# Attention feeding a mixture of experts: key splits, routing groups, softmax sums and filler matmuls rearranged

## The chip, the cores and the metric

The kernel runs on one core of one Trainium2 chip. The metric is device time in microseconds (us), the median of the timed runs; lower is better. The engines are PE (TensorE: matmuls; their weight loads are listed as PEld), DVE (VectorE), ACT (ScalarE), POOL (GpSimd) and SP (SyncE, which here only issues DMAs).

## The reference, cut to what matters

Random-feature attention (batch 4, 8 heads, sequence 576, head width 64, 128 features), whose output goes, as 2304 rows of 512, to a mixture of experts with one expert for each token (8 experts, hidden width 1024, at most 576 tokens for each expert).

```python
def phi(x):
    proj = einsum('bhsd,df->bhsf', x, w_phi)
    proj = proj - max(abs(proj), axis=-1, keepdims=True)
    return concatenate([exp(proj), exp(-proj)], axis=-1)
q_p, k_p = phi(q), phi(k)
kv = einsum('bhsf,bhsd->bhfd', k_p, v);  z = sum(k_p, axis=2)
num = einsum('bhsf,bhfd->bhsd', q_p, kv)
den = einsum('bhsf,bhf->bhs', q_p, z)[..., None] + 1e-06
x = (num / den).transpose(0, 2, 1, 3).reshape(2304, 512)

logits = x @ w_gate
expert_idx = argmax(logits, axis=1)
probs = exp(logits - max);  probs /= sum(probs) + 1e-09
gate_w = probs[arange(N), expert_idx]
# tokens of an expert in order of their number, at most `capacity` of them
h = maximum(einsum('ecd,edf->ecf', disp, w1), 0.0)
y = einsum('ecf,efd->ecd', h, w2)
out[i] = gate_w[i] * y[expert_idx[i], pos[i]]       # zero for tokens beyond capacity
```

## The kernel before, in words

**Attention.** The tokens are done in two halves (p = 0, 1) of nine blocks of 128 tokens. For each half there are 18 key items (head group g = 0, 1 of four heads, times nine blocks r), then 18 query items (block times head group). `attention` runs them as a software pipeline written out by hand: at step t, stage i of item t - i, in the order of stages 0, 2, 3, 1, then waiting folds, then 4 to 7. A key item: projection on PE (`project`), subtraction of the largest magnitude on DVE (`center`: a reduce at L198 and a subtraction at L202), two exponentials on ACT (`k_exp`, L239 and L240), sums over tokens on PE (`kv_sum`, L292), and after the last block of a sequence a fold of the sums. A query item: projection, `center`, transpose and two exponentials, the numerator and denominator on PE (`q_num`, L339), and for every second item `rows_out`, which divides by the denominator on DVE and writes the block's 128 rows of 512 into a tile xr, and the logits into a tile lg.

**Inputs of the projections.** Keys and queries come in chunks of 640 or 512 columns for a pair of heads (hp = 0 to 3). `x_load` issues a chunk's DMA on SP; `x_split` turns it into two f16 parts: ACT makes the high part (L167), POOL the rest by a subtraction (L168) one step later. The first four key chunks of head pairs 0 and 1 are used unsplit. `plan(chunks, marks)` gives each chunk a step, its mark: in that step its split is put into ACT's line, and one further chunk is loaded, in the order of a list whose first two loads are issued ahead of the loop, one at a time. SP issues DMAs in order; they take turns on eight semaphores, so that each waits for the one eight before it. In steps 3 to 26 SP also issues two DMAs a step that fill the expert buffer xs with a constant tile (`fill_xs`, L134 and L137), and from step 30 those that fill the output.

**Routing.** Blocks are routed in groups: when the last block of a group has its logits, `route` appends a list of 20 small steps to `pending`: sum of the logits over heads (L436), largest logit, one-hot choice of the expert, exponential (ACT), running counts (rb), positions within the expert by matmuls (PE, L417), the softmax sum (L448, L449: smx), the gate as its reciprocal, the slot number si, and the scatters. `tick`, which `center` and `rows_out` call between their operations, does one of these steps each time (more when many wait). Scatters of finished rows to xs in HBM are indirect DMAs on POOL (L421), one a step. Scratch for routing lies partly in SBUF tiles, partly in one PSUM bank, sm_t (`quick`), that also holds positions and folds. The last block's multiplication (block 17) is put into its group's list as an eleventh step.

**Seam and experts.** When nothing is pending any more, PE sums the counts, DVE writes cnt, and `warm(48)` (L214) issues 48 filler matmuls whose result is not used; the profile shows each as two passes. Then, in program order: load of expert 0's rows from xs (`load_x`, L623, five DMAs that wait for all scatters), `prep` of its first two tiles of 128 rows (PE transposes at L639, high part on ACT at L640, low part on DVE at L641), the splits of its first weights (`w_split`, eight parts, L111 on ACT and L112 on DVE; the weights were loaded during attention), and the eight experts. `ffn1` does for each of eight 128-column pieces f of the hidden layer twelve matmuls on 256 rows: four high by high (L650) and four low by high (L651) in turns, then four high by low (L653). `relu`, `ffn2` and a scaled scatter of the result into the output (`put`, L695 on POOL) follow; later experts' rows and splits are prepared during the one before.

Of the kernel before, what the change touches and what calls it, by code (L numbers as in the profile page):

```python
# [8 lines left out]
F32 = mybir.dt.float32  # L9
# [6 lines left out]
ALU = mybir.AluOpType  # L16
# [21 lines left out]
def tile_kernel(ctx: ExitStack, tc: tile.TileContext, qT, kT, vv, w_phi, w_g, w1, w2, out, cap):  # L38
# [84 lines left out]

    POS, SCR = 4 * GC, 4 * GC + 24
    sm_t = ps_1.tile([P, 512], F32, tag="sm", name="sm")
# [219 lines left out]
    grp = [None]  # L345

    def rows_out(p, r):
        blk = p * NBLK + r
        i, n = next((blk - g0, n) for g0, n in groups if g0 <= blk < g0 + n)
        if i == 0:  # L350
            grp[0] = (r_p.tile([P, n, XW], F32, tag=f"xr{n}", name="xr", bufs=(1, 1, 3)[n - 1]),
                      r_p.tile([P, n, H, NE], F32, tag="lg", name="lg", bufs=2))
        xr, lg = grp[0]
        num = num_t.pop((p, r))[:, :, 0:4 * GC].rearrange("p g (h c) -> p g h c", c=GC)
        rd = r_p.tile([P, 2, 4, 1], F32, tag="rd", name="rd")
        nc.vector.tensor_scalar(rd, num[:, :, :, D:VC], 1e-6, None, ALU.add)
        tick()
        nc.vector.reciprocal(rd, rd)
        tick()
        nc.vector.tensor_tensor(lg[:, i].rearrange("p (g h) e -> p g h e", g=2), num[:, :, :, VC:GC],  # L360
                                rd.to_broadcast([P, 2, 4, NE]), ALU.mult)
        if i == n - 1:
            route(blk - i, n, xr, lg)
        if blk == NT // P - 1:
            warm(8)
        else:
            tick()
        rows = xr[:, i, 0:DM].rearrange("p (g h d) -> p g h d", g=2, h=4)
        if blk == NT // P - 1:
            pending[-1].insert(10, lambda: nc.vector.tensor_tensor(  # L370
                rows, num[:, :, :, 0:D], rd.to_broadcast([P, 2, 4, D]), ALU.mult))
        elif p == 0 or r >= 7:
            nc.vector.tensor_tensor(rows, num[:, :, :, 0:D], rd.to_broadcast([P, 2, 4, D]), ALU.mult)
        else:
            nb = r_p.tile([P, 2, 4, D], F32, tag="nb", name="nb", bufs=2)
            nc.scalar.activation(nb, num[:, :, :, 0:D], AF.Copy)
            nc.gpsimd.tensor_tensor(rows, nb, rd.to_broadcast([P, 2, 4, D]), ALU.mult)
        tick()

    def route(blk, n, xr, lg):  # L380
        def small(name, shape, dt=F32):
            return r_p.tile([P, n, *shape], dt, tag=name, name=name)

        k = next(k for k, (g0, _) in enumerate(groups) if g0 == blk)
        room = [SCR + 96 * (k % 2)]

        def quick(w, each=n):
            a = room[0]
            room[0] += each * w
            assert room[0] <= SCR + 96 * (k % 2 + 1)  # L390
            return sm_t[:, a:room[0]].rearrange("p (n a) -> p n a", a=w)

        lt, sh, ix, sl, rn = quick(NE), quick(NE), quick(1), quick(1), quick(NE, 1)
        mx, ef = small("mx", [1]), small("ef", [NE])
        oh = small("oh", [NE], BF16)
        rb = r_p.tile([P, NE], BF16, tag="rb", name="rb")
        es, sel = small("es", [NE]), small("sel", [NE])
        sm, pr, ov = (small(x, [1]) for x in ("smx", "pr", "ov"))
        si = r_p.tile([P, n], I32, tag="si", name="si")
# [28 lines left out]
        def run_total():  # L428
            if old is None:
                v.tensor_copy(rb, rn[:, 0])  # L430
            else:
# [5 lines left out]
            lambda: v.tensor_reduce(flat(mx), lt, AX.X, ALU.max),  # L437
            lambda: v.tensor_tensor(sh, lt, mx.to_broadcast([P, n, NE]), ALU.subtract),
            lambda: v.scalar_tensor_tensor(ef, sh, 0.0, io, ALU.is_ge, ALU.mult),
            lambda: v.tensor_reduce(flat(ix), ef, AX.X, ALU.min),  # L440
            lambda: v.tensor_tensor(oh, ix.to_broadcast([P, n, NE]), io, ALU.is_equal),
            lambda: (v if late else nc.gpsimd).tensor_copy(xr[:, :, XW - 1:XW].bitcast(I32),
                                                           tokid[:, blk:blk + n].unsqueeze(2)),
            lambda: nc.scalar.activation(es, sh, AF.Exp),
            lambda: v.tensor_reduce(rn[:, 0], oh.rearrange("p n e -> p e n"), AX.X, ALU.add),
            run_total,
            positions,
            lambda: v.tensor_reduce(flat(sm), es, AX.X, ALU.add),  # L448
            lambda: v.tensor_scalar(sm, sm, 1e-9, None, ALU.add),  # L449
            lambda: v.tensor_tensor(sel, pos[0], oh, ALU.mult),  # L450
            lambda: v.reciprocal(xr[:, :, DM:DM + 1], sm),
            lambda: v.tensor_reduce(flat(pr), sel, AX.X, ALU.add),
# [6 lines left out]

    groups = [(0, 3), (3, 3), (6, 3), (9, 3), (12, 3), (15, 2), (17, 1)]  # L460

# [50 lines left out]
    def attention():  # L512
# [9 lines left out]
        order += [(K, 0, hp, 1) for hp in (0, 1)]  # L522
        plan([(K, 0, hp, c) for c in range(2) for hp in (2, 3)], [3, 5, 7, 9])
        plan([(Q, 0, hp, 0) for hp in range(4)], [10, 12, 13, 15])
        plan([(Q, 0, hp, 1) for hp in range(4)], [17, 19, 21, 23])
# [61 lines left out]
        nc.vector.tensor_scalar(cnt, tot, float(cap), None, ALU.min)  # L587
        warm(48)
        return cnt
# [176 lines left out]
    load_x(0)  # L766
    for t in ahead:
        prep(0, *t)
    for c in range(2):
        for part in range(4):  # L770
            w_split(0, c, part)
    prep_gi(0)
    for e in range(NE):
# [44 lines left out]
```

## Time and profile before

| | |
|---|---|
| timed runs | 477.46, 475.06, 474.16 us, median 475.06 us |
| profiled execution | 478.01 us, of which the span of instructions is 476.3 us |
| mean granted TensorE clock | 0.982 |
| busy share of the span: PE, DVE, ACT, POOL | 93%, 59%, 51%, 32% |
| bytes moved | 81.88 MB, mean 172 GB/s |
| chain that ended last, by engine | PE 53%, DVE 2%, DMA 2%, others 1% or less |

The page of the profile gives one execution. Attention lies from 0 to about 193 us, the experts from about 205 us to the end. A timeline row gives the start, the duration, the engine, the line, the operation with its output and inputs, how many instructions of it follow each other without a gap (x), and in brackets the engine's idle time before it and what ended that. PEclk is the granted TensorE clock as a share of full speed.

### The profile page before, as it was taken

What the parts mean: (1) busy time and instruction counts of PE and PEld (TensorE: products, weight loads), DVE (VectorE), ACT (ScalarE), POOL (GpSimd) and SP (SyncE); (2) the same over time, 40 slices, a digit from 0 to 9 for tenths busy, and PEclk for the clock granted to TensorE, in tenths of its full rate; (3) what the DMA queues carried; (4) which work ended last, traced back from release to release, by engine and by line L of the source; (5) the groups of instructions that cost most, each with busy time, mean ns of one, the idle gap of its engine ahead of it and who ended that gap; (6) DMA issues with size and microseconds to landing.
All of it is one profiled execution on the core that took longest, in us unless ns stands there. A gap on an engine that the chain in (4) does not pass through costs nothing.

```text
span 476.3 us, 11047 instructions
## 1 busy us (share of the span) xinstructions
PE 444.6 (93%) x4297; PEld 370.4 (78%) x4297; DVE 279.0 (59%) x621; ACT 244.6 (51%) x456; POOL 154.2 (32%) x181
## 2 busy tenths in 40 slices
PE   6599999988999999889899999999999999999993
PEld 4356688864557887879888979898989897989891
DVE  6256668998766888157742536666757570466121
ACT  3548766677775554057632425565656551454211
POOL 3449734679881426230211012121212120010101
PEclk9899999999999999889999999999999999999998
DMA  7986898842956002558762038495958570000000
GB/s 214 263 249 193 243 301 260 267 135 77 341 189 233 1 26 95 180 174 331 232 253 80 4 135 309 141 354 159 343 170 316 190 265 25 24 24 7 23 23 27
DMA packets 41993, 81.88 MB, mean 172 GB/s; under 512 B 3775, under 2 KB 6463, under 8 KB 41920
## 3 DMA queue, kind: packets, MB, share of 16 engines
q1 hardware_dynamic: 38816, 71.47, 46.2%
q0 software_dynamic: 3104, 9.46, 5.2%
q8 instruction: 43, 0.70, 0.6%
q14 instruction: 30, 0.25, 0.2%
HBM read 57.27 MB, written 24.30 MB: 171 GB/s over the span
## 4 chain that ended last, share of the span: by engine, by line
PE 53%; DVE 2%; DMA 2%; issue 1%; SPq 1%; ACT 1%; POOL 1%; another core or an unknown queue 0%; POOLq 0%; ACTq 0%
PE ph L650 9%; PE ph L651 9%; PE ph L653 9%; PE py L681 7%; PE py L682 7%; PE py L683 7%; PE pt L639 2%; PE py L679 1%; PE py L677 1%; DMA xi<-xs 1%; SPq L623 1%; DMA xs<-xr,si 1%; POOL xs L421 0%; DVE xl L641 0%; DVE l L112 0%
## 5 line engine op out<-in xcount | busy, mean ns | idle before, releaser
L650 PE MATMUL ph<-xh,h 128*128 128x256 f32 (+2 forms) x352 | 90.2, 287 | 5.0 <-ACT xh L640 1.6
L112 DVE TENSOR_TENSOR l<-raw,h 128x512 fp32r<-128x512 f32 x128 | 84.1, 690 | 13.1 <-ACT h L111 7.4
L651 PE MATMUL ph<-xh,l 128*128 128x256 f32 (+2 forms) x352 | 90.2, 287 | 0.7 <-DVE l L112 0.5
L695 POOL DMA_INDIRECT out<-y,it x22 | 23.6, 1073 | 195.6 <-ACT h L111 99.8
L168 POOL TENSOR_TENSOR stk<-px,stk 64x1280 f16<-64x1280 f32 (+1 forms) x28 | 66.5, 2377 | 43.2 <-ACT stk L167 33.2
L111 ACT ACTIVATE h<-raw 128x512 fp32r<-128x512 f32 x128 | 74.3, 626 | 0.0
L650 PEld LDWEIGHTS ph<-xh,h 128*128 128x128 f32 x352 | 68.0, 193 | 6.6 <-ACT xh L640 3.5
L667 DVE SCALAR_TENSOR_TENSOR h<-ph,h 128x256 fp32r<-128x256 f32 (+1 forms) x112 | 38.4, 360 | 53.8 <-ACT h L664 53.7
L651 PEld LDWEIGHTS ph<-xh,l 128*128 128x128 f32 x352 | 68.0, 193 | 1.7 <-DVE l L112 1.5
L664 ACT ACTIVATE h<-ph 128x256 fp32r<-128x256 f32 (+2 forms) x88 | 33.3, 379 | 60.7 <-PE ph L653 49.9
L198 DVE TENSOR_REDUCE m<-pr 128x4 f32<-128x512 f32 x72 | 49.5, 687 | 20.5 <-PE pr L188 11.4
L681 PE MATMUL py<-h,h 128*128 128x512 f32 x152 | 60.1, 395 | 0.0
L682 PE MATMUL py<-l,h 128*128 128x512 f32 x152 | 59.3, 390 | 0.0
L683 PE MATMUL py<-h,h 128*128 128x512 f32 x152 | 59.3, 390 | 0.0
L653 PE MATMUL ph<-xl,h 128*128 128x256 f32 (+2 forms) x352 | 57.3, 285 | 0.0
L202 DVE TENSOR_TENSOR d<-pr,m 128x512 f32<-128x512 f32 x72 | 49.8, 692 | 7.8 <-ACT kp L240 4.1
L653 PEld LDWEIGHTS ph<-xl,h 128*128 128x128 f32 x352 | 49.3, 193 | 0.0
L641 DVE TENSOR_TENSOR xl<-pt,xh 128x512 fp32r<-128x512 f32 (+1 forms) x23 | 14.3, 653 | 55.7 <-ACT xh L640 42.0
L292 PE MATMUL acc<-kp,v 128*64 128x256 f32 (+1 forms) x320 | 40.5, 401 | 5.2 <-ACT kp L240 4.9
L339 PE MATMUL acc<-kv,qp 128*64 128x73 f32 x1152 | 44.4, 229 | 0.0
L339 PEld LDWEIGHTS acc<-kv,qp 128*64 128x64 f32 x1152 | 39.1, 136 | 5.9 <-issue 5.4
L640 ACT ACTIVATE xh<-pt 128x512 fp32r<-128x512 f32 (+1 forms) x23 | 12.1, 568 | 59.0 <-PE pt L639 28.5
(103 smaller groups left out, 691.3 us busy)
## 6 DMA issues: line engine op xcount, KB each, us to landing
raw<-in_w SPq DMA_DIRECT2D x32, 1024.0 KB, 7.5
xi<-xs SPq DMA_DIRECT2D x32, 257.0 KB, 5.1
xs<-fill SPq DMA_DIRECT2D x24, 257.0 KB, 5.8
out<-fill SPq DMA_DIRECT2D x18, 256.0 KB, 6.5
xs<-fill SPq DMA_DIRECT2D x24, 128.5 KB, 5.3
px<-in_kT SPq DMA_DIRECT2D x10, 256.0 KB, 6.7
px<-in_qT SPq DMA_DIRECT2D x8, 320.0 KB, 5.0
v<-in_vv SPq DMA_DIRECT2D x1, 2304.0 KB, 13.4
```

The costliest lines, as they stand in the source:

```text
L111: nc.scalar.activation(hi[:, part], t[:, part], AF.Copy)
L112: nc.vector.tensor_tensor(lo[:, part], t[:, part], hi[:, part].bitcast(F32), ALU.subtract)
L168: return lambda: nc.gpsimd.tensor_tensor(t[D:P], x, t[0:D], ALU.subtract)
L198: nc.vector.tensor_reduce(m.rearrange("p a b -> p (a b)"), pr, AX.X, ALU.max, apply_absolute_value=True)
L202: nc.vector.tensor_tensor(d, pr, m.to_broadcast([P, 4, NF]), ALU.subtract)
L339: nc.tensor.matmul(num[lo:hi, g, j * GC:(j + 1) * GC], qp[:, a, j, lo:hi], kv_t[b][:, a, 4 * g + j], start=(a == 0), stop=(a == 1))
L650: nc.tensor.matmul(acc, hi[:, k, fs], xh[:, k, o:o2], start=(k == 0), stop=False)
L651: nc.tensor.matmul(acc, lo[:, k, fs], xh[:, k, o:o2], start=False, stop=False)
L653: nc.tensor.matmul(acc, hi[:, k, fs], xl[:, k, o:o2], start=False, stop=(k == 3))
L681: nc.tensor.matmul(py[0:m], h_t[f][:, s0:s0 + m], hi, start=(f == 0), stop=False)
L682: nc.tensor.matmul(py[0:m], h_t[f][:, s0:s0 + m], lo, start=False, stop=False)
L683: nc.tensor.matmul(py[0:m], h_t[f][:, at:at + m], hi, start=False, stop=(f == 7))
```

## The change

Six edits, all in the kernel's body:

1. The marks of the first half's split chunks move: keys from steps 3, 5, 7, 9 to 5, 6, 8, 10, the first four query chunks from 10, 12, 13, 15 to 11, 12, 14, 15. The loads that hang on them move too.
2. Routing groups of the first half (blocks 0 to 8) are 4 and 5 blocks instead of 3, 3 and 3. All blocks of a half write their rows into one tile; the logits' tiles are named by group size.
3. In `route`, the softmax sum goes from an SBUF tile (smx) to the PSUM scratch (sm); the shifted logits overwrite the logits (sh is gone); the reciprocal stands ahead of the product with the one-hot.
4. Block 17's rows are multiplied by ACT, one operation for each head, instead of one DVE operation.
5. The eight splits of expert 0's first weights stand ahead of its rows' `prep`.
6. 28 filler matmuls instead of 48.

```diff
-    POS, SCR = 4 * GC, 4 * GC + 24
+    POS, SCR, SW = 4 * GC, 4 * GC + 40, 80
...
+    xr_t = r_p.tile([P, NBLK, XW], F32, tag="xr", name="xr", bufs=1)
...
-            grp[0] = (r_p.tile([P, n, XW], F32, tag=f"xr{n}", name="xr", bufs=(1, 1, 3)[n - 1]),
-                      r_p.tile([P, n, H, NE], F32, tag="lg", name="lg", bufs=2))
+            grp[0] = (xr_t[:, blk % NBLK:blk % NBLK + n],
+                      r_p.tile([P, n, H, NE], F32, tag=f"lg{n}", name="lg", bufs=2 if n == 3 else 1))
...
         if blk == NT // P - 1:
-            pending[-1].insert(10, lambda: nc.vector.tensor_tensor(
-                rows, num[:, :, :, 0:D], rd.to_broadcast([P, 2, 4, D]), ALU.mult))
+            for h in range(H):
+                nc.scalar.activation(rows[:, h // 4, h % 4], num[:, h // 4, h % 4, 0:D], AF.Copy,
+                                     scale=rd[:, h // 4, h % 4])
...
-        lt, sh, ix, sl, rn = quick(NE), quick(NE), quick(1), quick(1), quick(NE, 1)
+        lt, ix, sl, rn, sm = quick(NE), quick(1), quick(1), quick(NE, 1), quick(1)
...
-        sm, pr, ov = (small(x, [1]) for x in ("smx", "pr", "ov"))
+        pr, ov = small("pr", [1]), small("ov", [1])
...
-            lambda: v.tensor_tensor(sh, lt, mx.to_broadcast([P, n, NE]), ALU.subtract),
+            lambda: v.tensor_tensor(lt, lt, mx.to_broadcast([P, n, NE]), ALU.subtract),
...
             lambda: v.tensor_reduce(flat(sm), es, AX.X, ALU.add),
             lambda: v.tensor_scalar(sm, sm, 1e-9, None, ALU.add),
+            lambda: v.reciprocal(xr[:, :, DM:DM + 1], sm),
             lambda: v.tensor_tensor(sel, pos[0], oh, ALU.mult),
-            lambda: v.reciprocal(xr[:, :, DM:DM + 1], sm),
...
-    groups = [(0, 3), (3, 3), (6, 3), (9, 3), (12, 3), (15, 2), (17, 1)]
+    groups = [(0, 4), (4, 5), (9, 3), (12, 3), (15, 2), (17, 1)]
...
-        plan([(K, 0, hp, c) for c in range(2) for hp in (2, 3)], [3, 5, 7, 9])
-        plan([(Q, 0, hp, 0) for hp in range(4)], [10, 12, 13, 15])
+        plan([(K, 0, hp, c) for c in range(2) for hp in (2, 3)], [5, 6, 8, 10])
+        plan([(Q, 0, hp, 0) for hp in range(4)], [11, 12, 14, 15])
...
-        warm(48)
+        warm(28)
...
     load_x(0)
-    for t in ahead:
-        prep(0, *t)
     for c in range(2):
         for part in range(4):
             w_split(0, c, part)
+    for t in ahead:
+        prep(0, *t)
```

In the rows below, a name with a number is one buffer; the lines of the changed kernel lie two or three behind those of before.

On ACT, right behind the exponentials of key items 0 and 1, there stood before (px is a loaded chunk, stk its split, d the centred projection of an item, kp its exponentials; items 2 to 5):

```order
L167 ACTIVATE stk_189<-px_147 64x1280
L239 ACTIVATE kp_196<-d_185 128x4x128
L240 ACTIVATE kp_196<-d_185 128x4x128
L239 ACTIVATE kp_215<-d_207 128x4x128
L240 ACTIVATE kp_215<-d_207 128x4x128
L167 ACTIVATE stk_232<-px_149 64x1280
L239 ACTIVATE kp_239<-d_228 128x4x128
L240 ACTIVATE kp_239<-d_228 128x4x128
L239 ACTIVATE kp_260<-d_252 128x4x128
L240 ACTIVATE kp_260<-d_252 128x4x128
L167 ACTIVATE stk_286<-px_187 64x1024
```

In the changed kernel there stands, from the second exponential of item 2 on:

```order
L240 ACTIVATE kp_193<-d_186 128x4x128
L239 ACTIVATE kp_211<-d_204 128x4x128
L240 ACTIVATE kp_211<-d_204 128x4x128
L167 ACTIVATE stk_228<-px_148 64x1280
L239 ACTIVATE kp_235<-d_224 128x4x128
L240 ACTIVATE kp_235<-d_224 128x4x128
L167 ACTIVATE stk_253<-px_150 64x1280
L239 ACTIVATE kp_260<-d_248 128x4x128
L240 ACTIVATE kp_260<-d_248 128x4x128
L239 ACTIVATE kp_290<-d_282 128x4x128
L240 ACTIVATE kp_290<-d_282 128x4x128
L167 ACTIVATE stk_303<-px_226 64x1024
```

The first chunk's split (stk_189, now stk_228) moved behind the exponentials of items 2 and 3, the second's behind those of item 4, and the third's (stk_286, now stk_303) behind those of items 5 and 6.

On SP, behind the DMAs of the first key chunks, there stood before (fill is the constant tile, v the values):

```order
L175 DMA v_140<-in_vv 128x9x256
L160 DMA px_187<-in_kT 64x2x512
L134 DMA xs_66<-fill_129 128x514
L137 DMA xs_66<-fill_129 64x514
L134 DMA xs_66<-fill_129 128x514
L137 DMA xs_66<-fill_129 64x514
L160 DMA px_230<-in_kT 64x2x512
```

In the changed kernel:

```order
L175 DMA v_141<-in_vv 128x9x256
L134 DMA xs_66<-fill_129 128x514
L137 DMA xs_66<-fill_129 64x514
L134 DMA xs_66<-fill_129 128x514
L137 DMA xs_66<-fill_129 64x514
L160 DMA px_226<-in_kT 64x2x512
L134 DMA xs_66<-fill_129 128x514
L137 DMA xs_66<-fill_129 64x514
L160 DMA px_251<-in_kT 64x2x512
```

The third chunk's load moved behind two fills of two DMAs each; the fourth stands one fill behind it instead of two.

On DVE, from block 17's softmax sum to the first expert, there stood before (l0 and l1 are the low parts of the weights):

```order
L449 TENSOR_SCALAR smx_2980<-smx_2980 128x1
L450 TENSOR_TENSOR sel_2979<-sm_128,oh_2976 128x8
L451 RECIPROCAL xr_2964<-smx_2980 128x1
L452 TENSOR_REDUCE pr_2981<-sel_2979 128x1
L453 SCALAR_TENSOR_TENSOR sm_128<-sm_128,pr_2981 128x1
L454 TENSOR_SCALAR ov_2982<-pr_2981 128x1
L455 SCALAR_TENSOR_TENSOR si_2983<-sm_128,ov_2982 128x1
L587 TENSOR_SCALAR cnt_3034<-sm_128 128x8
L641 TENSOR_TENSOR xl_3113<-pt_3156,xh_3112 128x4x128
L641 TENSOR_TENSOR xl_3113<-pt_3157,xh_3112 128x4x128
L112 TENSOR_TENSOR l0_3105<-raw_1893,h0_3104 128x512 x4
L112 TENSOR_TENSOR l1_3107<-raw_2027,h1_3106 128x512 x4
```

In the changed kernel:

```order
L452 TENSOR_SCALAR sm_128<-sm_128 128x1
L453 RECIPROCAL xr_132<-sm_128 128x1
L454 TENSOR_TENSOR sel_2938<-sm_128,oh_2935 128x8
L455 TENSOR_REDUCE pr_2939<-sel_2938 128x1
L456 SCALAR_TENSOR_TENSOR sm_128<-sm_128,pr_2939 128x1
L457 TENSOR_SCALAR ov_2940<-pr_2939 128x1
L458 SCALAR_TENSOR_TENSOR si_2941<-sm_128,ov_2940 128x1
L590 TENSOR_SCALAR cnt_2999<-sm_128 128x8
L112 TENSOR_TENSOR l0_3050<-raw_1853,h0_3049 128x512 x4
L112 TENSOR_TENSOR l1_3052<-raw_1993,h1_3051 128x512 x4
L644 TENSOR_TENSOR xl_3058<-pt_3101,xh_3057 128x4x128
L644 TENSOR_TENSOR xl_3058<-pt_3102,xh_3057 128x4x128
```

The softmax sum has changed from smx to sm, the reciprocal stands ahead of the product, and the eight weight splits stand ahead of the rows' low parts (L641, now L644).

## Rows read from the trace of the kernel before

**Rows 1.** Timeline of PE, early part of attention

```profile
19.97 1.98 PE L292 MATMUL acc<-kp,v 128*64 128x256 f32 x8 [4.86 <-ACT kp L240]
...
31.73 0.23 PE L192 MATMUL pr<-whi,stk 128*128 128x128 f16 x1
...
34.42 1.08 PE L292 MATMUL acc<-kp,v 128*64 128x256 f32 x8
```

**Rows 2.** Busy time by stretch, all engines (columns in the first line)

```profile
core 0: us, PE busy (x) PEld busy (x) DVE busy (x) ACT busy (x) POOL busy (x), PEclk, DMA share, GB/s
20.00:30.00 10.00, 10.00 (x74) 4.72 (x75) 3.40 (x5) 6.67 (x11) 8.46 (x4) 0.70 0.86 261
80.00:110.00 30.00, 25.51 (x495) 21.57 (x490) 27.41 (x81) 19.91 (x34) 21.62 (x14) 1.00 0.66 195
195.00:196.00 1.00, 1.00 (x6) 1.00 (x6) 0.00 (x0) 0.00 (x0) 0.00 (x0) 0.50 0.64 247
```

**Rows 3.** Timeline of POOL from the last scatters on

```profile
193.84 0.97 POOL L421 DMA_INDIRECT xs<-xr,si  x1 [0.30 <-issue]
200.35 0.19 POOL L633 COPY gt<-xi 128x1 f32<-128x1 f32 x1 [5.53 <-DMA xi<-xs]
...
231.38 1.28 POOL L695 DMA_INDIRECT out<-y,it  x1 [20.68 <-ACT h L111]
```

**Rows 4.** Timeline of PE at the seam

```profile
192.93 12.59 PE L214 MATMUL pt<-ident 128*128 128x128 f32 x96
205.63 1.07 PE L639 MATMUL pt<-ident,xi 128*128 128x128 f32 x8
...
211.96 0.41 PE L650 MATMUL ph<-xh,h 128*128 128x256 f32 x1
...
214.16 0.28 PE L650 MATMUL ph<-xh,h 128*128 128x256 f32 x1
214.28 0.28 PE L651 MATMUL ph<-xh,l 128*128 128x256 f32 x1
```

**Rows 5.** Timeline of ACT, early part of attention

```profile
9.84 0.61 ACT L240 ACTIVATE kp<-d 128x512 f32<-128x512 f32 x1
17.61 1.27 ACT L167 ACTIVATE stk<-px 64x1280 f16<-64x1280 f32 x1 [7.15 <-DMA px<-in_kT]
...
24.35 1.06 ACT L167 ACTIVATE stk<-px 64x1024 f16<-64x1024 f32 x1 [0.16 <-DMA px<-in_kT]
```

**Rows 6.** Timeline of POOL, query items of the first half

```profile
98.26 2.61 POOL L168 TENSOR_TENSOR stk<-px,stk 64x1280 f16<-64x1280 f32 x1 [0.79 <-PE pr L193]
```

**Rows 7.** DMA issues on the page (count, KB each, us to landing)

```profile
xs<-fill SPq DMA_DIRECT2D x24, 257.0 KB, 5.8
...
xs<-fill SPq DMA_DIRECT2D x24, 128.5 KB, 5.3
```

**Rows 8.** Timeline of DVE, query items of the first half

```profile
76.88 0.51 DVE L436 TENSOR_REDUCE sm<-lg 128x24 f32<-128x192 f32 x1
...
82.75 0.19 DVE L445 TENSOR_REDUCE sm<-oh 128x8 f32<-128x24 bf16 x1 [1.42 <-ACT es L444]
...
84.97 0.96 DVE L449 TENSOR_SCALAR smx<-smx 128x3 f32<-128x3 f32 x1
...
98.63 0.69 DVE L202 TENSOR_TENSOR d<-pr,m 128x512 f32<-128x512 f32 x1
99.24 1.66 DVE L449 TENSOR_SCALAR smx<-smx 128x3 f32<-128x3 f32 x1
```

**Rows 9.** Instructions of L449 (duration ns: min/median/max, first and last start)

```profile
L449 DVE TENSOR_SCALAR smx<-smx x7: 154/520/1656, 85.0 to 192.0; 128x3 f32<-128x3 f32 x5, 128x2 f32<-128x2 f32 x1, 128x1 f32<-128x1 f32 x1
```

**Rows 10.** Timelines of ACT and DVE at the seam

```profile
206.34 1.08 ACT L640 ACTIVATE xh<-pt 128x512 fp32r<-128x512 f32 x2 [15.47 <-DMA xi<-xs]
207.31 4.26 ACT L111 ACTIVATE h<-raw 128x512 fp32r<-128x512 f32 x8
...
206.97 1.29 DVE L641 TENSOR_TENSOR xl<-pt,xh 128x512 fp32r<-128x512 f32 x2 [13.69 <-DMA xi<-xs]
208.18 4.90 DVE L112 TENSOR_TENSOR l<-raw,h 128x512 fp32r<-128x512 f32 x8
```

More of the change, by code (lines that the diff above doesn't have):

```diff
@@ L384, in route @@
         k = next(k for k, (g0, _) in enumerate(groups) if g0 == blk)
-        room = [SCR + 96 * (k % 2)]
+        room = [SCR + SW * (k % 2)]
         def quick(w, each=n):
@@ L389, in quick @@
             room[0] += each * w
-            assert room[0] <= SCR + 96 * (k % 2 + 1)
+            assert room[0] <= SCR + SW * (k % 2 + 1) <= 512
             return sm_t[:, a:room[0]].rearrange("p (n a) -> p n a", a=w)
-        lt, sh, ix, sl, rn = quick(NE), quick(NE), quick(1), quick(1), quick(NE, 1)
+        lt, ix, sl, rn, sm = quick(NE), quick(1), quick(1), quick(NE, 1), quick(1)
         mx, ef = small("mx", [1]), small("ef", [NE])
@@ L437, in route @@
             lambda: v.tensor_reduce(flat(mx), lt, AX.X, ALU.max),
-            lambda: v.tensor_tensor(sh, lt, mx.to_broadcast([P, n, NE]), ALU.subtract),
-            lambda: v.scalar_tensor_tensor(ef, sh, 0.0, io, ALU.is_ge, ALU.mult),
+            lambda: v.tensor_tensor(lt, lt, mx.to_broadcast([P, n, NE]), ALU.subtract),
+            lambda: v.scalar_tensor_tensor(ef, lt, 0.0, io, ALU.is_ge, ALU.mult),
             lambda: v.tensor_reduce(flat(ix), ef, AX.X, ALU.min),
@@ L443, in route @@
                                                            tokid[:, blk:blk + n].unsqueeze(2)),
-            lambda: nc.scalar.activation(es, sh, AF.Exp),
+            lambda: nc.scalar.activation(es, lt, AF.Exp),
             lambda: v.tensor_reduce(rn[:, 0], oh.rearrange("p n e -> p e n"), AX.X, ALU.add),
```

## The prediction

> **What bounds it now.** I read the page of the profile first (PE is busy almost everywhere), then the busy time in stretches, then PE's waits, then the timelines of the other engines where PE has holes. The holes are three. In the first 30 us PE stands still once for 4.86 us [rows 1], and from 20 to 30 us it is busy throughout, but at a granted clock that averages 0.70 [rows 2]: of the two levels, 2.4 and 1.2 GHz, six of these ten microseconds had the lower, and a stretch bound by PE lost 3.0 us by it. From 80 to 110 us PE is idle for 30 - 25.51 = 4.5 us, while DVE is busy for 27.4 of the 30 [rows 2]. The third hole is the seam to the experts, from the last scatter at 193.84 [rows 3] to the third f of the first expert at 214.16 [rows 4], f being one of the eight 128-column pieces of the hidden layer. So the sum is made of three places; the other edits are costed behind them.
>
> **Place 1, key splits later.** ACT ends the exponentials of item 1 at 9.84 + 0.61 = 10.45, and what it does next is the split of the first 640-column key chunk, which starts only at 17.61, when that chunk has landed [rows 5]. The exponentials of items 2 and 3 stand behind it, and PE's hole of 4.86 us ends when they come [rows 1]. Afterwards they are ahead of the split (order rows above), so hole and half-clock stretch go: PE is 4.86 + 3.0 = 7.9 us earlier. The same wait at the head of ACT's line can come back at the next splits, so I follow each. First chunk: its load is not moved, ACT splits it from 17.61 to 18.88 and does the next two exponentials, 0.61 each [rows 5], until 20.1. Second chunk: POOL's two subtractions of 2.61 [rows 6] follow from about 19.0 and end at 24.3; PE needs them for item 9, whose projection at 31.73 [rows 1] moves to 31.73 - 7.9 = 23.8: half a microsecond of waiting. Third chunk (512 columns): its load is moved on SP behind two fills, 2 x (257.0 + 128.5) KB [rows 7], and at the 261 GB/s that the queues moved from 20 to 30 us [rows 2] they take 3.0 us. It landed at 24.35 [rows 5], so now at 27.3. ACT splits it for 1.06 [rows 5], until 28.4, and does the exponentials of item 7 until 29.5; PE's sum for item 7, now at 34.42 [rows 1], would else start at 26.5. So PE waits 3 us there, and from then on it is 34.42 - 29.5 = **4.9 us** early, which I take. The fourth chunk and the query chunks move by one fill or none, and ACT comes to them later than they land. Bounds: 7.9 if the third chunk lands in time; 1.9 if the new 3 us hole is followed by half clock as the old one was (3.0 more).
>
> **Place 2, routing in the first half.** Per group, routing runs some 19 small DVE operations between the row work; two groups lie in the stretch where DVE is the limit, afterwards one. A small operation lasts 0.19 [rows 8] and overlaps the next; at half of that, 18 of them and the 0.51 of the reduction over heads [rows 8] are 2.2 us. Then the sum of the softmax: its tensor_scalar on smx lasts between 154 and 1656 ns [rows 9]. The longest starts at 99.24 and ends at 100.90 [rows 8]; POOL's subtraction runs from 98.26 to 100.87 [rows 6]. The DVE subtraction that reads PSUM at 98.63, inside the same POOL operation, takes 0.69 for 512 columns [rows 8]. So the operation whose tensors lie in SBUF alone waited for POOL's, and the one that reads PSUM did not. In the changed kernel this sum is read and written in PSUM. The two long ones in this stretch, 0.96 and 1.66 [rows 8], would be 0.15 each: 2.3 us less. DVE thus gains 4.5, less 0.2 because the reduction over heads grows by a third. PE's holes there are 4.5 and no more can come back; some of them wait for a group's positions, which one group in place of two still needs, so I take three quarters, **3.4 us**. Not less than 1.1: only the removed group counts, and half of it was hidden.
>
> No row shows that operation with both tensors in PSUM. The Trainium skill, VectorE: DVE Perf Modes, section Why PSUM operands drop a tier, says that a PSUM operand closes the mode which takes both SBUF read ports, and SBUF — State Buffer, section Who interferes with whom, that only such modes and operations with two SBUF inputs meet POOL. By that rule the whole 2.3 us go; the rows alone would leave anything from 0 to 2.3.
>
> **Place 3, the seam.** Of the 96 filler passes (48 matmuls of two passes) 56 stay. All take 12.59 us from 192.93, so 0.131 each [rows 4], and 56 take 7.3; but the first of them run at half clock (0.50 at 195 to 196 [rows 2]) and all of those stay, so I take 7.7: the filler ends at 200.6. The expert's first rows have landed at 200.35, where POOL's copy of them starts [rows 3]. So the transposes start at 200.6 instead of 205.63 [rows 4]: 5.0 us. The splits of the first weights take ACT 4.26 and DVE 4.90 us for eight [rows 10], now behind the rows, afterwards in the empty time before them: ACT's are done by 192.93 + 4.26 = 197.2 if they start with the filler, DVE's, behind cnt, which waits for the matmul ahead of the filler, go from 193.3 to 198.2. Both are hidden as long as that is before the rows' own work. Then the first f waits for rows alone: xh is done 206.34 + 1.08 - 205.63 = 1.8 after the transposes start, xl 2.6 [rows 10]. Eight matmuls at the 0.12 that two starts lie apart at full clock [rows 4] end at 2.75, four more at 3.25; the second f starts then, where it was 211.96 - 205.63 = 6.3 [rows 4] after them: 3.1 us. It takes 12 x 0.12 = 1.44 instead of 214.16 - 211.96 = 2.2 [rows 4], if the clock is not halved: 0.75. Together **8.8 us**. Bounds: 9.1 if the filler ends with the rows, 6.4 by rival B below.
>
> **Edits that I cost at nothing.** Multiplying block 17's rows moves from DVE to eight ACT operations, each on an eighth of 512 columns: between 8 x 0.07 and 8 x 0.54 (an eighth and all of ACT's pass over 512 columns, half of the row at 206.34 [rows 10]). I take 1.5 us, nearest to the short end since the columns are few, in an ACT that has hardly other work left. DVE's time there is not on the chain: the last scatter's row names nothing but its own issue as what it waited for [rows 3]. At 4.3 us the last exponential and with it the last scatter could come up to 2.8 later; that lies in the range. One tile for all rows makes second-half rows wait for first-half scatters, which end some 30 us before. Larger groups scatter later, far from a reader.
>
> **Sum.** 4.9 + 3.4 + 8.8 = 17.1. The profiled execution took 478.0 us (span 476.3 and 1.7 around it), so it would take 460.9. It lies 2.95 above the median of the timed runs, 475.06, so the median goes to **458**.
>
> **Rivals.**
> A. The early hole only moves: half clock behind the wait at item 7, 3.0 us, 461. For it: that is what followed the old hole [rows 1, 2]. Against: the new one is three fifths as long. Chance 0.17.
> B. DVE's early splits hold up POOL's last scatters. A scatter that ran beside such splits took 1.28 instead of 0.97 [rows 3], 0.3 more; at most each of the two last scatters waits out one whole subtraction, 4.90 / 8 = 0.61 [rows 10]. Then rows land 1.2 later, the filler hides 0.3 of it, and PE, idle for 0.9, may start the expert at the half clock of today: 2.2 instead of 1.44 in each of two f, 1.5. 458 + 2.4 = 460.4, chance 0.12. The Trainium skill, SBUF — State Buffer, section Who interferes with whom, gives this rule: a DVE operation with two SBUF inputs keeps POOL from reading for the whole instruction. By it the delay is the 1.2, by the scatter's row 0.6.
> C. DVE's debt is moved and not paid: the group of five does at the border to the second half what the removed group did, and PE waits there for those 2.2 us. 460.2, chance 0.12.
> D. The other side: the third key chunk, now behind two fills, lands much later, and ACT holds every exponential behind its split. Each microsecond after 27.3 is one on PE; from 44 on nothing is left of the gain, from 49 the kernel is over 1% slower. Against it speak 0.77 MB at 261 GB/s [rows 2, 7]. 475 and more, chance 0.06.
> E. The third chunk lands in time and place 1 gives its 7.9: 455, chance 0.10.
>
> **Numbers.** The forecast has 0.43. A and B together give 463.4, with half of C 464.5; E with the upper bounds of places 2 and 3 gives 454. 8 in 10 lie from 454 to 464.5. A measurement of this kernel tells about 1% from no change. Faster by more: all but D, 0.94; within 1%: 0.04; slower: 0.02.
>
> **What would show it.** ACT's exponentials of items 2 and 3 before 14 us, and PE without a hole from 15 to 20; one wait of PE near 27 us on kp, ended by the third split's end. No softmax sum over 0.3 us, and PE busy over 0.95 in the q stretch of the first half. A filler of about 7.7 us, the transposes within 0.5 us of its end, the first f 1.9 us later, all eight splits done before. Wrong would be: a wait for the third chunk above 5 us, a scatter over 1.6 us beside the splits, or a stretch at 0.50 behind the transposes.

## The result and the profile after

| | before | after |
|---|---|---|
| timed runs, median | 475.13 us (474.16 to 477.46) | 459.81 us (459.27 to 460.40) |
| profiled execution, span | 478.01, 476.3 us | 459.27, 457.6 us |
| mean granted clock | 0.982 | 0.990 |

The ratio of the times is 0.9668, with a 95% interval of 0.9634 to 0.9701: 15.3 us less between the medians, where 17.1 was forecast (458.0, range 454 to 464.5). Between the two profiled executions it is 18.7 us. Measured again among later runs, the ratio was 0.9715 (0.9650 to 0.9781).

Where the 18.7 us of the traces lie is read by landmarks, each the start of an operation that both kernels have: DVE's reduce (L198) of items 24, 45 and 71, the filler's first matmul, the first transpose of expert 0's rows, its second and third f.

| stretch | before | after | gain | forecast |
|---|---|---|---|---|
| start to item 24 (place 1) | 69.51 | 61.95 | 7.56 | 4.9 |
| item 24 to 45 (place 2) | 49.03 | 46.06 | 2.97 | 3.4 |
| item 45 to 71 | 64.24 | 63.99 | 0.25 | 0 |
| item 71 to the filler | 10.15 | 10.31 | -0.16 | 0 |
| filler to the transposes | 12.70 | 8.22 | 4.48 | 5.0 |
| transposes to the second f | 6.33 | 3.38 | 2.95 | 3.1 |
| second to third f | 2.20 | 1.44 | 0.76 | 0.75 |
| third f to the end | 262.14 | 262.25 | -0.11 | 0 |

The stretches of after that answer to [rows 2] (columns as there):

```profile
core 0: us, PE busy (x) PEld busy (x) DVE busy (x) ACT busy (x) POOL busy (x), PEclk, DMA share, GB/s
20.00:30.00 10.00, 9.79 (x113) 5.54 (x114) 6.39 (x10) 6.50 (x11) 7.20 (x4) 1.00 1.02 303
80.00:110.00 30.00, 29.02 (x484) 21.13 (x486) 27.14 (x70) 22.62 (x37) 24.99 (x14) 1.00 0.48 139
184.00:186.00 2.00, 2.00 (x12) 2.00 (x11) 2.00 (x5) 0.67 (x2) 0.43 (x1) 0.53 0.41 156
```

The clock is at its full level from 20 to 30 us, where it was 0.70, and PE's idle time from 80 to 110 fell from 4.5 to 1.0 us. Taken by items, from 24 to 45, it fell from 4.49 (49.03 less 44.54 busy) to 1.59 us (46.06 less 44.47). The filler still begins at half clock, that is at the lower of the two levels.

Timeline of ACT early in after, for [rows 5]:

```profile
12.70 0.61 ACT L240 ACTIVATE kp<-d 128x512 f32<-128x512 f32 x1
15.44 1.27 ACT L167 ACTIVATE stk<-px 64x1280 f16<-64x1280 f32 x1 [2.12 <-DMA px<-in_kT]
...
24.48 1.06 ACT L167 ACTIVATE stk<-px 64x1024 f16<-64x1024 f32 x1 [3.50 <-DMA px<-in_kT]
...
25.97 0.61 ACT L240 ACTIVATE kp<-d 128x512 f32<-128x512 f32 x1
```

The exponentials of items 2 and 3 are done at 13.3, ahead of the first split, which also starts 2.2 us earlier than before. The third chunk's split starts at 24.48, as before (24.35), and not at 27.3. So PE has next to no hole there. Timeline of PE in after, at the third chunk, at the border of the halves and at the seam, for [rows 1, 4]:

```profile
26.63 1.08 PE L292 MATMUL acc<-kp,v 128*64 128x256 f32 x8 [0.21 <-ACT kp L240]
...
98.96 0.22 PE L192 MATMUL pr<-whi,stk 128*128 128x128 f16 x1 [0.98 <-DVE sm L443]
...
182.31 8.12 PE L214 MATMUL pt<-ident 128*128 128x128 f32 x56
190.53 1.06 PE L642 MATMUL pt<-ident,xi 128*128 128x128 f32 x8
192.38 0.39 PE L653 MATMUL ph<-xh,h 128*128 128x256 f32 x1 [0.79 <-ACT xh L643]
...
193.91 0.28 PE L653 MATMUL ph<-xh,h 128*128 128x256 f32 x1
```

The matmuls of L292 that stood at 34.42 come at 26.63. PE's wait of 0.98 at the border of the halves is not new. Before the change the same matmul waited longer there (timeline of PE in before):

```profile
109.78 0.22 PE L192 MATMUL pr<-whi,stk 128*128 128x128 f16 x1 [1.62 <-DVE sm L440]
```

The filler's 56 passes take 8.1 us; the first f starts 1.85 us behind the transposes, waits for rows alone, and runs without a gap.

Timeline of POOL, ACT and DVE at the seam, for [rows 3, 10]:

```profile
183.21 1.22 POOL L424 DMA_INDIRECT xs<-xr,si  x1 [0.30 <-ACT h L111]
189.90 0.19 POOL L636 COPY gt<-xi 128x1 f32<-128x1 f32 x1 [5.47 <-DMA xi<-xs]
...
180.40 4.27 ACT L111 ACTIVATE h<-raw 128x512 fp32r<-128x512 f32 x8 [0.16 <-ACT es L447]
...
182.88 4.90 DVE L112 TENSOR_TENSOR l<-raw,h 128x512 fp32r<-128x512 f32 x8 [0.23 <-ACT h L111]
```

The splits are over at 187.8, 2.7 us before the transposes. The last scatter took 1.22 instead of 0.97 us beside them, and the rows land 6.69 us after its start (6.51 before).

### The profile page after: what moved, and what is told of

It is laid out like the page before. It is cut to its first block, busy times and chain, and to the rows that moved or that the text cites. A ratio compares the mean times of both kernels' runs of the same rounds, so it can differ in the third digit from the quotient of the medians.

```text
span 457.6 us, 10959 instructions
## 1 busy us (share of the span) xinstructions
PE 434.8 (95%) x4256; PEld 362.5 (79%) x4256; DVE 275.5 (60%) x604; ACT 246.1 (54%) x463; POOL 156.6 (34%) x180
## 4 chain that ended last, share of the span: by engine, by line
PE 55%; issue 3%; DVE 2%; ACT 1%; another core or an unknown queue 0%; ACTq 0%; POOL 0%; POOLq 0%
PE ph L653 10%; PE ph L656 9%; PE ph L654 9%; PE py L684 7%; PE py L685 7%; PE py L686 7%; PE pt L642 2%; PE py L682 1%; PE py L680 1%; ACT xh L643 1%; ACT h L111 0%; PE pt L214 0%; ACT y L695 0%; DVE half L693 0%
## 5 line engine op out<-in xcount | busy, mean ns | idle before, releaser
L653 PE MATMUL ph<-xh,h 128*128 128x256 f32 (+2 forms) x352 | 89.2, 285 | 4.1 <-ACT xh L643 2.4
L654 PE MATMUL ph<-xh,l 128*128 128x256 f32 (+2 forms) x352 | 88.8, 284 | 0.0
L198 DVE TENSOR_REDUCE m<-pr 128x4 f32<-128x512 f32 x72 | 49.4, 687 | 15.9 <-PE pr L193 8.0
L644 DVE TENSOR_TENSOR xl<-pt,xh 128x512 fp32r<-128x512 f32 (+1 forms) x23 | 14.2, 652 | 46.1 <-ACT xh L643 46.0
L292 PE MATMUL acc<-kp,v 128*64 128x256 f32 (+1 forms) x320 | 39.1, 391 | 0.4 <-ACT kp L240 0.4
```

Of the source, the lines that this page charges most:

```text
L198: nc.vector.tensor_reduce(m.rearrange("p a b -> p (a b)"), pr, AX.X, ALU.max, apply_absolute_value=True)
L653: nc.tensor.matmul(acc, hi[:, k, fs], xh[:, k, o:o2], start=(k == 0), stop=False)
L654: nc.tensor.matmul(acc, lo[:, k, fs], xh[:, k, o:o2], start=False, stop=False)
```

## The experiments

All of them are judged by time and by the landmarks of their traces, since single executions of one kernel differ by several microseconds (of 18 further runs of the kernel before, the lowest is 472.39 and the highest 478.88). A ratio is to the kernel before timed beside them, with its 95% interval. The first four were timed against a median of 475.52 for the kernel before, the second four against 481.26, the last four against 474.32.

**Place 1 alone, and its two halves.** `marks_only` is the kernel before with the new marks:

```diff
-        plan([(K, 0, hp, c) for c in range(2) for hp in (2, 3)], [3, 5, 7, 9])
-        plan([(Q, 0, hp, 0) for hp in range(4)], [10, 12, 13, 15])
+        plan([(K, 0, hp, c) for c in range(2) for hp in (2, 3)], [5, 6, 8, 10])
+        plan([(Q, 0, hp, 0) for hp in range(4)], [11, 12, 14, 15])
```

> The kernel before with the new marks alone (loads and splits of the first half's chunks). Theory: place 1 is worth all of the 7.6 us that the trace of after is ahead by item 21 (its reduce on DVE starts at 54.2 instead of 61.7), and the rest of the trace is as before; span 468.7. The conversion is what is open: if the 2.9 us by which the profiled execution of before exceeds the median lay in the early half-clock stretch, the median gain here is only 4.7 (470.4) and the runs lie within 1.2 us; rival: they lay at the seam, so the median is 467.5 and the runs still spread over 3 us.

Measured: 470.50 us (468.92 to 472.60), 5.0 less than before between medians (ratio 0.9920, 0.9876 to 0.9965); item 24 at 61.54, 7.97 us earlier in the trace, which is that of the fastest of its six executions. In the other two, loads and splits are taken apart: `loads_late` has only the loads at the new steps, `splits_late` only the splits.

```diff
-            for x in at.get(t, []):
+            for _ in range(sum(m == t for m in [5, 6, 8, 10, 11, 12, 14, 15]) if t < 16 else len(at.get(t, []))):
                 more_load()
```

This is `loads_late`, with the marks of before; `splits_late` has the new marks and in this line the old steps, 3, 5, 7, 9, 10, 12, 13, 15.

> The kernel before with the chunks' loads at the new steps (third chunk behind two fills) and the splits at the old ones. Theory 1 (the order of loads matters by itself): the first chunk's split starts near 15.4 instead of 17.6, PE's hole shrinks by 2.2 us, time 2 to 3 us less. Rival (only the order on ACT matters): split at 17.6 as before, hole 4.9, time within 0.5 us of before.

Measured: 476.49 us (472.59 to 478.67), no difference that can be told (ratio 1.0025, 0.9993 to 1.0058). Its traced execution was the fastest of its ten and has item 24 at 65.53, 3.98 us earlier, with the first split at 14.87 and a hole of 1.98 us on PE (timelines of ACT and PE):

```profile
14.87 1.27 ACT L167 ACTIVATE stk<-px 64x1280 f16<-64x1280 f32 x1 [4.16 <-DMA px<-in_kT]
...
17.23 1.98 PE L292 MATMUL acc<-kp,v 128*64 128x256 f32 x8 [1.98 <-ACT kp L240]
```

> The kernel before with the splits at the new steps and the loads at the old ones (third chunk ahead of the fills). Theory 1 (the order of loads gives 2.2 us of the gain): first chunk's split at 17.6, PE waits 2 to 3 us for item 4's exponentials, time 4.5 to 5.5 us less than before. Rival (only the order on ACT matters): no PE hole over 0.5 us, all of the 7.6 us as with both.

Measured: 471.14 us (469.60 to 472.31), 4.4 less (ratio 0.9913, 0.9877 to 0.9948); item 24 at 62.56, 6.95 us earlier. The first chunk lands later than in any other trace here, and PE does not wait for it (timelines of ACT and PE):

```profile
11.49 1.08 PE L292 MATMUL acc<-kp,v 128*64 128x256 f32 x8 [0.71 <-DMA v<-in_vv]
...
18.24 1.27 ACT L167 ACTIVATE stk<-px 64x1280 f16<-64x1280 f32 x1 [4.61 <-DMA px<-in_kT]
...
18.28 1.08 PE L292 MATMUL acc<-kp,v 128*64 128x256 f32 x8
```

So place 1 is the order on ACT, the rival to theory 1: with the splits behind the exponentials PE does not wait, although the chunk lands at 18.2. Of the 1.02 us by which item 24 is later than in `marks_only`, 0.71 is a wait for v, the first line above, and not for a chunk. The order of the loads, from which I expected a new 3 us hole, costs nothing. In the traces of all kernels the first chunk's split starts at 14.87 to 17.33 with the new order of loads (eleven traces) and at 17.15 to 18.24 with the old (three). Whether that gives time while the splits stand early stays open: the one trace of `loads_late` says up to 4 us, its ten times say nothing.

**Place 3 alone.** `seam_only` is the kernel before with expert 0's splits ahead of its rows and 28 fillers.

```diff
-        warm(48)
+        warm(28)
...
-    for t in ahead:
-        prep(0, *t)
     for c in range(2):
         for part in range(4):
             w_split(0, c, part)
+    for t in ahead:
+        prep(0, *t)
```

> The kernel before with expert 0's splits ahead of its rows and 28 filler matmuls, nothing else. Theory: 8.2 us less from the start of the filler to the second f (12.2 instead of 19.0 us to it, then 1.44 instead of 2.2); median 466.9 and runs that spread over 3 us, since the early half-clock stretch remains. Rival: the 2.9 us of the profiled execution lay at the seam, median 469.8 and runs within 1.2 us.

Measured: 468.45 us (467.75 to 471.40), 7.1 less between medians (ratio 0.9880, 0.9854 to 0.9905). From the filler to the transposes 8.15 us, first f 1.85 us behind them, as in the changed kernel. Where the 2.9 us of the profiled execution lay is not settled by this. `marks_only` has the median of the guess that they lay early (470.4), `seam_only` one between its two (466.9 and 469.8), and with one place undone or the other, runs spread over 3.7 us.

**Place 3, its two halves in the changed kernel.** `splits_behind` has the splits behind `prep` again, `filler_48` the 48 fillers.

```diff
+    for t in ahead:
+        prep(0, *t)
     for c in range(2):
         for part in range(4):
             w_split(0, c, part)
-    for t in ahead:
-        prep(0, *t)
```

> The changed kernel with expert 0's weight splits behind its rows again, 28 fillers. Theory: transposes at the same time (190.5), but the second f 6.3 instead of 3.4 us after them and itself up to 2.2 long: 3.0 to 3.7 us slower, 463 to 463.5; and the last scatter back to 0.97 us from 1.22. Rival: the clock stays full in the first two f (the filler ends closer to them), then 3.0.

Measured: 471.41 us (470.59 to 472.32). Timeline of PE at its seam:

```profile
198.98 1.06 PE L642 MATMUL pt<-ident,xi 128*128 128x128 f32 x8
201.35 0.38 PE L653 MATMUL ph<-xh,h 128*128 128x256 f32 x1 [1.30 <-ACT h L111]
...
202.27 0.58 PE L654 MATMUL ph<-xh,l 128*128 128x256 f32 x1 [0.54 <-DVE l L112]
...
205.31 0.41 PE L653 MATMUL ph<-xh,h 128*128 128x256 f32 x1
```

The second f is 6.33 us behind the transposes, to the hundredth what it was before, and the third 2.56 us behind that (207.87), at half clock (granted clock 0.50 from 202 to 208 us). Against the changed kernel's 4.82 from the transposes to the third f these are 8.89: 4.1 us, a little over what I expected. The last scatter is back to 0.98 us.

And the other:

```diff
-        warm(28)
+        warm(48)
```

> The changed kernel with 48 filler matmuls again. Theory: the rows wait for the filler: 40 passes more at 0.11 are 4.5 us, 464.3, with the first f the same 1.85 us behind the transposes. Rival: the filler was hidden behind the rows' landing, under 1 us.

Measured: 472.28 us (471.87 to 473.34). The filler takes 12.7 us to the transposes instead of 8.2, and nothing behind it changes:

```profile
191.92 12.59 PE L214 MATMUL pt<-ident 128*128 128x128 f32 x96
204.61 1.06 PE L642 MATMUL pt<-ident,xi 128*128 128x128 f32 x8
206.46 0.39 PE L653 MATMUL ph<-xh,h 128*128 128x256 f32 x1 [0.79 <-ACT xh L643]
```

**Place 2, its two halves in the changed kernel.** `sum_in_sbuf` has the softmax sum in an SBUF tile, `groups_of_3` the first half in groups of 3.

```diff
-        lt, ix, sl, rn, sm = quick(NE), quick(1), quick(1), quick(NE, 1), quick(1)
+        lt, ix, sl, rn = quick(NE), quick(1), quick(1), quick(NE, 1)
...
-        pr, ov = small("pr", [1]), small("ov", [1])
+        sm, pr, ov = (small(x, [1]) for x in ("smx", "pr", "ov"))
```

> The changed kernel with the softmax sum back in an SBUF tile, reciprocal still ahead. Theory 1 (the sum in PSUM is most of place 2): the tensor_scalar lasts 0.5 us or more wherever POOL works beside it, and the trace is 1.0 to 1.5 us behind the changed one by item 45 (gain 9.5 where it is 10.5 to 10.8). Rival (the removed group is most of it): it is behind by under 0.4 us, time within 0.5 us of 459.8.

```diff
-    groups = [(0, 4), (4, 5), (9, 3), (12, 3), (15, 2), (17, 1)]
+    groups = [(0, 3), (3, 3), (6, 3), (9, 3), (12, 3), (15, 2), (17, 1)]
```

> The changed kernel with the first half's groups of 3 again, all else as changed, the sum in PSUM. Theory 1 (PSUM is most): by item 45 within 1.0 us of the changed kernel. Rival (the removed group is most): 1.8 to 2.5 us behind it, time 461.8. In both no softmax sum above 0.3 us.

Measured: 468.22 us (466.94 to 469.51) and 468.30 us (466.71 to 469.06). These two ran, with the two before them, while engines made pauses that the other traces do not have; `splits_behind`, whose attention is that of the changed kernel, shows them on DVE and ACT:

```profile
96.74 0.69 DVE L198 TENSOR_REDUCE m<-pr 128x4 f32<-128x512 f32 x1 [2.22 <-remote]
...
175.51 0.60 ACT L326 ACTIVATE qp<-pt 128x512 f32<-128x512 f32 x1 [2.59 <-remote]
```

So the landmarks decide, up to where the pauses begin (item 33) and with them named behind that (`groups_of_3` has none before item 45). In us:

| kernel | item 24 to 33 | item 33 to 45 |
|---|---|---|
| before; marks_only | 23.69; 23.68 | 25.34; 25.33 |
| groups_of_3 | 22.93 | 25.00 |
| sum_in_sbuf | 23.41 | 25.63 (DVE pauses 0.99 and 1.46) |
| after; after_again | 22.63; 22.63 | 23.43; 23.45 |
| splits_behind | 22.63 | 26.66 (DVE pause 2.22) |

Up to item 33 the sum in PSUM is worth 0.78 (23.41 to 22.63) and the groups 0.30 (22.93 to 22.63). The 0.78 is the one long tensor_scalar, which again ends with POOL's subtraction (DVE to 83.18, POOL to 83.15):

```profile
82.24 0.94 DVE L452 TENSOR_SCALAR smx<-smx 128x4 f32<-128x4 f32 x1
...
81.01 2.14 POOL L168 TENSOR_TENSOR stk<-px,stk 64x1024 f16<-64x1024 f32 x1 [2.07 <-ACT stk L167]
```

With the sum in PSUM, all six last 0.16 us in the changed kernel (for [rows 9]):

```profile
L452 DVE TENSOR_SCALAR sm<-sm x6: 157/160/167, 81.8 to 181.1; 128x3 f32<-128x3 f32 x2, 128x4 f32<-128x4 f32 x1, 128x5 f32<-128x5 f32 x1, 128x2 f32<-128x2 f32 x1
```

Up to item 45 groups of 3 are 1.87 us behind (47.93 to 46.06), and `groups_of_3` is 1.1 ahead of before (49.03), which is what the sum in PSUM gives with groups of 3: 0.76 up to item 33, 0.34 behind it. With groups of 4 and 5 the sum's share at item 45 cannot be told: `sum_in_sbuf` and `splits_behind` are level there (49.04 and 49.29) with pauses of about the same size. So both halves count, the removed group more, as the rival in the expectation of `groups_of_3` had it (1.8 to 2.5 us).

**The changed kernel again, and three beside it.**

> The changed kernel itself, so that the three beside it have it on the same chip. Ratio to before as first measured, 0.967 within 0.004; what differs from the first trace is pauses that no edit explains (half clock in the filler, an engine that waits for no other engine's work), up to 3 us in all.

Measured: 460.64 us (459.35 to 461.81). The distances between its landmarks from item 24 to 71 are those of the first trace within 0.05 us.

The changed kernel has a wait on DVE that before had too: the counts rn lie in the PSUM bank that ACT's exponential es reads, and DVE writes them behind es, which itself stands behind ACT's other work. All instructions of L448 in after (what its engine sat idle for ahead of them: us in all, times):

```profile
its engine sat idle before it (us, times) until:
  ACT es L447: 5.1, 4
```

The two longest on the timeline:

```profile
79.52 0.21 DVE L448 TENSOR_REDUCE sm<-oh 128x8 f32<-128x32 bf16 x1 [1.28 <-ACT es L447]
...
158.06 0.19 DVE L448 TENSOR_REDUCE sm<-oh 128x8 f32<-128x24 bf16 x1 [1.78 <-ACT es L447]
```

`counts_in_sbuf` takes the counts out of that bank:

```diff
-        lt, ix, sl, rn, sm = quick(NE), quick(1), quick(1), quick(NE, 1), quick(1)
+        lt, ix, sl, sm = quick(NE), quick(1), quick(1), quick(1)
+        rn = r_p.tile([P, 1, NE], F32, tag="rn", name="rn")
...
-        warm(28)
+        warm(26)
```

> The changed kernel with each group's counts (rn) in an SBUF tile, and 26 fillers. In the changed kernel DVE waits four times, 5.1 us in all (1.28 at 79.52, 1.78 at 158.06), for ACT's exponential es, which reads the PSUM bank that rn is written to. Theory 1 (that wait is what is left of DVE's debt): those waits go, PE's holes at rb (0.61 and 0.51) and the 0.98 at the border shrink, 1 to 2 us less than the changed kernel, 0.4 of it by the filler. Rival: PE's position matmuls write the same bank and wait for es in DVE's place, so only the filler's 0.4 is seen.

Measured: 458.42 us (457.66 to 460.24), 2.2 below the changed kernel beside it. From item 24 to 71 it takes 107.33 us instead of 110.09. PE's matmuls for the positions now wait for es, but shortly (0.16 us at 79.49), and its wait at the border stays. At the seam 1.9 us of this are lost again. The last scatter starts 12.32 us behind item 71 instead of 11.20, so the rows land later. The filler, here at full clock (its 52 passes take 6.05 us), ends 1.87 us before they do, and the expert starts at half clock (granted clock 0.50 from 190 to 192 us). The transposes come 18.98 us behind item 71 instead of 18.36, and the first result's scatter 23.35 us behind them instead of 22.11 (timeline of PE):

```profile
79.49 0.18 PE L421 MATMUL sm<-oh,tri 128*128 128x32 bf16 x1 [0.16 <-ACT es L448]
...
188.22 1.12 PE L643 MATMUL pt<-ident,xi 128*128 128x128 f32 x8 [1.87 <-DMA xi<-xs]
190.07 0.58 PE L654 MATMUL ph<-xh,h 128*128 128x256 f32 x1 [0.73 <-ACT xh L644]
```

It is the fastest kernel of the study, if by less than four runs of each can settle (458.42 to 460.64, and the runs overlap).

> The same, and the rows of blocks 4 and 5 are multiplied as the second half's are: copied by ACT (0.60), multiplied on POOL (1.03), off DVE (0.68 each). Theory 1 (DVE's throughput limits 80 to 100): up to 1.0 us less than counts_in_sbuf. Rival: ACT's copies delay the exponentials behind them by 0.6 each and nothing is gained, or 0.5 is lost.

Beside the edits of `counts_in_sbuf`:

```diff
-        elif p == 0 or r >= 7:
+        elif (p == 0 and r not in (4, 5)) or r >= 7:
```

Measured: 460.24 us (459.41 to 461.07); item 24 to 33 takes 21.50 us, with the rows on DVE 21.45. Nothing is gained: DVE's throughput was no longer the limit there once the wait for es was gone. PE is idle for 0.16 us of that stretch in both kernels, so there was nothing left for DVE to give.

`filler_0_row17` is the changed kernel without the filler and with block 17's rows multiplied by DVE, as before.

```diff
-            for h in range(H):
-                nc.scalar.activation(rows[:, h // 4, h % 4], num[:, h // 4, h % 4, 0:D], AF.Copy,
-                                     scale=rd[:, h // 4, h % 4])
+            pending[-1].insert(10, lambda: nc.vector.tensor_tensor(
+                rows, num[:, :, :, 0:D], rd.to_broadcast([P, 2, 4, D]), ALU.mult))
...
-        warm(28)
```

> The changed kernel without the filler at the seam (8 warm matmuls in the last routing remain), and block 17's rows multiplied by DVE again. Theory: PE stands still for 7.5 us until the rows land, starts the expert at half clock and loses 1.9 to 3.5 us there (first and second f at 0.18 or more for each matmul instead of 0.12); transposes no earlier than 0.6 us before those of the changed kernel; net 1.5 to 3 us slower. Rival: the clock is at its full level once PE works again, then 0.5 faster. Block 17: from its first DVE operation to cnt 4.9 us (4.7 before, 5.0 after); rival: the ACT version is ahead.

Measured: 460.59 us (459.40 to 461.46), the same as the changed kernel beside it. Its trace shows the loss all the same (timeline of PE):

```profile
189.95 1.94 PE L640 MATMUL pt<-ident,xi 128*128 128x128 f32 x8 [7.18 <-DMA xi<-xs]
192.57 0.58 PE L651 MATMUL ph<-xh,h 128*128 128x256 f32 x1 [0.69 <-ACT xh L641]
...
195.30 0.41 PE L651 MATMUL ph<-xh,h 128*128 128x256 f32 x1
...
197.65 0.28 PE L651 MATMUL ph<-xh,h 128*128 128x256 f32 x1
```

From 184 to 196 us the granted clock is 0.50; the third f starts 7.70 us behind the transposes, in the changed kernel 4.83. Against that the transposes come 0.5 earlier (17.83 us behind item 71 instead of 18.36). The net 2.3 us should show in the time and do not, and why is open. From the third f to the end this trace is the shorter by 1.2 to 2.0 us; pauses of 0.5 to 0.9 us among the experts, which the changed kernel's two traces have and this one has not, are a part of that. What the 28 matmuls are worth is thus between 0 and 2.3 us. Block 17: from its first DVE operation to cnt 5.39 us with DVE, 5.19 with ACT, so the rival (ACT ahead) holds, but the last scatter starts 5.91 us behind it in both.

## Why the prediction was right, and where it was not

**Place 1.** The mechanism was right (exponentials behind a split that waits for its chunk, then half clock), and `splits_late` shows that the order on ACT carries the gain without the loads (4.4 of 5.0 us between medians, whose runs overlap). The step that failed is "its load is moved on SP behind two fills ... so now at 27.3": the chunk's split started at 24.48, and the 3 us hole at item 7 was 0.21 us. I added the time of the fills' bytes to the landing, as if the transfers went one after the other. But the load's issue was over only 1.8 us later (at 14.28 instead of 12.50), and from there it took 10.2 us to the split where it had taken 11.9. Timelines of SP, before and after:

```profile
8.45 4.05 SPq L160 DMA_DIRECT2D px<-in_kT  x1
...
13.63 0.65 SPq L160 DMA_DIRECT2D px<-in_kT  x1
```

So several transfers are under way at once, and the chunk was not held by those just ahead of it. The other traces agree: this split waits for its chunk in all fourteen, and starts at 22.77 to 25.76 in the eleven with two fills ahead of the load, at 24.00 to 24.35 in the three without. In the trace place 1 gave 7.6 us, near its upper bound of 7.9 (rival E), instead of 4.9.

**Place 2.** 3.4 forecast, 2.97 by item 45 and 3.2 by item 71. Both terms exist; the removed group gives 1.9 (2.2 less 0.2 forecast), the sum in PSUM about 1.1 (2.3 forecast). The sum was oversized since it was costed by the whole length of its two waits. The first, 0.8 us too long, came back nearly whole (0.76), but of the 1.5 us of the second only 0.34 did; what hid the rest is not shown. The Trainium skill's rule (SBUF — State Buffer, section Who interferes with whom), that a DVE operation in a mode which takes both SBUF ports and an operation of POOL shut each other out for the whole instruction, agrees with the traces: in SBUF the sum waits for the end of POOL's operation (0.94 us), in PSUM never (0.157 to 0.167). Rival C did not come: PE's wait at the border, 0.98 us, had been 1.62 before.

**Place 3.** 8.8 forecast, 8.2 measured. The step that was off is "so I take 7.7" for the 56 passes: 8.1. The price of 0.131 for a pass was an average over passes at both clock levels. In both traces some 17 passes at the start run at half clock, 0.213 us apart, and the rest 0.112 apart. So the 40 passes left out were all at 0.112, 4.5 us (12.59 less 8.12 is 4.47), where 7.7 counts on 4.9, and the extra of the half clock stayed whole. The transposes then came 0.6 us after the rows' landing and not with it. Order of the splits: 3.7 (2.95 and 0.76), 0.15 under the forecast (3.1 and 0.75), and without a stretch at half clock behind the transposes. Rival B: the last scatter took 0.25 us longer beside the splits, near the row's 0.3 and not 0.61, and the filler hid it. In the nine traces with the splits ahead it takes 1.21 to 1.47 us, in the other five 0.97 or 0.98. So the splits do slow it, but the 1.2 us that the prediction names as the delay by the rule of whole instructions did not come.

**Edits costed at nothing.** Block 17 on ACT took 1.75 us (1.5 forecast) and moved the last scatter by nothing (11.20 us behind item 71 in the changed kernel with ACT and, in `filler_0_row17`, with DVE). So the 0.16 us lost from item 71 to the filler are not its.

**The step from the trace to the median.** Here two errors cancel in part, and that 458 lies so near 459.8 is to that extent luck. The sum was 1.6 us too small for the traces (17.1, measured 18.7). Then the 2.95 us by which the profiled execution of before lay above its median were taken off the forecast as if the changed kernel's would lie as far above; it lies 0.5 below, an error of 3.5 us the other way. So the gain between medians, 15.3, is 1.8 below the sum. Where the excess sat is shown in part: the same early code reached item 24 at 69.51 in before and at 68.65 in `seam_only`, and the same 96 passes took 12.70 us to the transposes in before and `splits_late` but 11.07 in `marks_only` and `loads_late`. The change removes the early hole; the filler's half clock it does not, as its own trace shows. Alone, the two large places gave 5.0 and 7.1 us between medians (3.8 and 5.7 by the ratios) where the traces show 7.6 and 8.2.

## What to carry to other kernels

An instruction that waits for a transfer belongs behind all work that its engine could do until then; what counts is the order on that engine, and a transfer that is issued behind a few others need not land later by the time of their bytes. A price read from one traced execution holds for that execution: where a stretch runs at half clock, look at several traces of the same code before its excess is carried to the median. A price averaged over passes at two clock levels does not hold for a part of them. When a scratch bank is shared by two engines, look for waits between operations that use different columns of it: here a tile in SBUF for the counts gave 2.8 us up to item 71 in the trace, more than the 1.1 of the edit to the sum, though 1.1 of the 2.8 were gone again by the last scatter.

## What the runs showed that I had not expected

DVE's count waited up to 1.78 us for ACT's exponential, which reads other columns of the same PSUM bank. The Trainium skill (PSUM — Partial Sum Buffer, section PSUM bank collisions raise a hardware error) says why two engines' accesses to a bank are kept apart: the hardware does not arbitrate them. The trace agrees in so far as the wait goes once the counts lie elsewhere.

In one group of runs every traced execution had pauses of 1 to 2.6 us on ACT or DVE whose releaser is given as remote, and the kernel before took 481.26 us there instead of 474 to 476; no other trace has one in attention. What they wait for the profile does not show.
